# Six layer-1 steps of the fifth and sixth group as 128-token products, and one pair of weight sums placed later

## The chip, the cores and the metric

The kernel runs on one core of a Trainium2 chip. Its metric is the device time of one execution, in microseconds (us), here as a median over several executions. A core has five engines that work side by side, each through its own list of instructions in order: TensorE (PE in the profile, its weight loads PEld), VectorE (DVE), ScalarE (ACT), GpSimd (POOL) and SyncE (SP, which here only starts DMAs). They wait for one another on semaphores.

## The reference

Two layers, one behind the other, over 4 sequences of 768 tokens with 8 heads of 64 features.

```python
# linear attention with decay, in blocks of 64 tokens
intra = einsum('bhic,bhjc->bhij', qb, kb) * Dmask     # lower triangle of lam**(i-j)
intra = einsum('bhij,bhjd->bhid', intra, vb)
inter = einsum('bhid,bhde->bhie', qb * lam_pow, kv_state)
out   = intra + inter
kv_state = lam_block * kv_state + einsum('bhsd,bhse->bhde', kb_dec, vb)
# then, with the heads side by side as x of 512 features
xn = (x - mean) / sqrt(var + 1e-6) * g_ln
y  = x + maximum(xn @ w_ch1, 0) @ w_ch2               # 512 -> 2048 -> 512
```

Inputs and output are float32; the kernel multiplies in bfloat16 and float16 and adds in float32.

## The kernel before

The 3072 tokens are cut into 12 units of 256 tokens, numbered u = 0 to 11. A unit passes through the attention, gives normalised and transposed activations `xT`, and is then a group g = u of the two-layer network (`mlp(g)`, L524). The fifth group is g = 4, the sixth g = 5.

Nothing is ordered by a scheduler. The lower part of the kernel (from L961) is one long list, written by hand, of loads, attention stages and "units": `units(n)` (L1044) takes the next n steps of the list `plan` (L1028 to L1040) and emits them. Each engine executes its share of the list in the order of the text.

*Layer 1.* Group g has eight layer-1 steps. In the usual form, `m1` (L531), a step fills one PSUM bank with two blocks of 128 hidden features for all 256 tokens: 2 blocks times 4 slices of the 512 inputs, 8 products of 128x128 weights with 256 columns (L539), and one ACT instruction that applies the maximum and writes `hT` (L542). In the other form, `m1_tile(c, i)` (L643), a step takes four feature blocks for the 128 tokens of half i: 16 products with 128 columns (L650) and an ACT instruction of the same size (L653). Four tile steps for c in (2, 3) and i in (0, 1) do the work of the last four usual ones. Every product is a weight load and a matmul, two PE instructions.

*Layer 2.* Groups 0 to 3 multiply `hT` by `w2` directly (`m2`, L659: four steps per 128 tokens, four products of 512 columns each at L676), and DVE adds the scaled result to x (`finish`, L700). Groups 4 to 11 replace eight block products by seven (`m2w`, L636, products P1 to P7 into the banks pwa to pwd at L574). These need sums of blocks of W2, which `w_sums(c, n)` (L792) puts into `wt[c]` once for each of the four pieces c of W2: n = 0 gives two of the four sums of a piece (L798, L799), n = 1 the other two (L801, L802), all on DVE. They also need sums of the hidden activations, `h_sums` (L549), again on DVE.

*Attention.* For units 6 to 11 the stage `X(u)` (L943; `X1` and `X2` for u = 6) puts four runs of small 64x64 products one behind the other on PE: `av64` and `inter` of unit u-1, `kv64` and `scores64` of unit u. Unit u's transposed `kqT` and most `xT` come through DMA transposes started by SP.

All PSUM results of the network and of `kv64` share one tag, "mm", with four banks that go round: a product into a bank waits until the instruction that read its last content is done.

Of the kernel before, what the change touches and what calls it, by code (L numbers as in the profile page):

```python
# [17 lines left out]
def kernel(  # L18
# [773 lines left out]
    def w_sums(c, n):  # L792
        v = w2[c].rearrange("p (k e) d -> p k e d", e=2)
        w = DM // 2
        b11, b12, b21, b22 = v[:, :, 0, 0:w], v[:, :, 0, w:], v[:, :, 1, 0:w], v[:, :, 1, w:]
        t1, t2, t3, t4 = (wt[c][:, :, i] for i in range(4))
        if n == 0:
            nc.vector.tensor_tensor(t1, b12, b11, op=ALU.subtract)  # L798
            nc.vector.tensor_tensor(t3, b12, b22, op=ALU.add)  # L799
        else:  # L800
            nc.vector.tensor_tensor(t2, b11, t3, op=ALU.subtract)  # L801
            nc.vector.tensor_tensor(t4, t2, b21, op=ALU.add)  # L802
# [225 lines left out]
    plan = [(m1b, n) for n in range(m1b.count // 2, m1b.count)]  # L1028
    plan += [(m2, i, part) for part in range(KB // 4) for m2, i in ((m2a, 0), (m2a, 1), (m2b, 0))]
    plan += [(m2b, 1, part) for part in range(KB // 4)]  # L1030
    for g in range(2, len(groups)):
        m1, m2 = mlp(g)
        if g == 3:
            plan += [(m1, n) for n in range(4)] + [(m1.tile, c, i) for c in (2, 3) for i in range(2)]
        else:
            plan += [(m1, n) for n in range(m1.count)]
        if g >= WG:
            plan += [(m2.w, n) for n in range(8)]
        else:
            plan += [(m2, i, part) for i in range(len(groups[g])) for part in range(KB // 4)]  # L1040
# [3 lines left out]
    def units(n):  # L1044
        for _ in range(n):
            f, *a = next(steps)
            f(*a)
# [55 lines left out]
    in_v(4, nc.gpsimd)  # L1103
    units(3)
    w_sums(0, 0)
    w_sums(0, 1)
    units(2)
    w_sums(1, 0)
    units(3)
    s12(3)  # L1110
# [265 lines left out]
```

## Time and profile before

| | |
|---|---|
| time before, median of 3 runs | 211.05 us (209.8, 211.05, 211.47) |
| the profiled execution's own time | 209.97 us |
| its span in the profile | 208.3 us |
| PE busy | 197.5 us (95%), 3179 products and as many weight loads |
| DVE, ACT, POOL busy | 136.2 us, 120.8 us, 85.7 us |
| PE clock granted | full in all 40 slices |
| layer-1 products, usual form (L539) | 688 |
| layer-1 products, tile form (L650) | 160 |
| DMA queue q8, instructions | 25 packets, 0.41 MB |

The span is the stretch from the first to the last recorded instruction; the execution takes 1.7 us more. Times within the profile are counted from the start of the span. A busy PE is not a PE at its peak, since the ends of matmuls are modelled: where the text gives a rate of products, it is taken from the starts of two neighbouring runs.

### The profile page before, as it was taken

Reading aid. Unit: us, or ns where it says so; the run is one execution under the profiler, and the core shown is the slowest. Engines: PE = TensorE matmul, PEld = TensorE weight load, DVE = VectorE, ACT = ScalarE, POOL = GpSimd, SP = SyncE. Lnnn points to the kernel's source line nnn. Section 1 sums busy time; section 2 is a strip of 40 time slices with the busy share of each in tenths; the row PEclk is TensorE's granted clock in tenths of the full one; section 3 lists DMA queues with packets and bytes.
Section 4 is the critical chain, followed back from the end, with each engine's and each line's share of the span. In section 5 each row is a group of like instructions: output and inputs, shape, how many; then the busy total and the mean of one; then the engine's idle time right before and its main releaser. Section 6 shows DMA issues by size and latency. Waiting matters only on the chain.

```text
span 208.3 us, 7396 instructions
## 1 busy us (share of the span) xinstructions
PE 197.5 (95%) x3179; PEld 157.9 (76%) x3179; DVE 136.2 (65%) x277; ACT 120.8 (58%) x278; POOL 85.7 (41%) x118
## 2 busy tenths in 40 slices
PE   4989999999999999999999999999799999999991
PEld 2468798454775686588888888888588888888880
DVE  3588543437865659786887874848947947855262
ACT  3776577444466378085665866575486665752620
POOL 5658059118663531663275424753552202011020
PEclk9999999999999999999999999999999999999999
DMA  4999999999899999999899999798995020168303
GB/s 109 301 250 222 177 273 161 206 295 266 206 208 284 219 164 170 185 214 216 179 198 184 191 191 182 198 184 172 195 139 130 6 50 0 30 164 241 127 18 88
DMA packets 91011, 36.41 MB, mean 175 GB/s; under 512 B 65121, under 2 KB 88161, under 8 KB 90978
## 3 DMA queue, kind: packets, MB, share of 16 engines
q1 hardware_dynamic: 86368, 31.53, 75.0%
q0 software_dynamic: 4224, 4.19, 12.9%
q8 instruction: 25, 0.41, 0.8%
q10 hardware_dynamic: 386, 0.20, 0.4%
q14 instruction: 8, 0.07, 0.1%
HBM read 27.27 MB, written 6.29 MB: 161 GB/s over the span
## 4 chain that ended last, share of the span: by engine, by line
PE 81%; DMA 6%; DVE 5%; ACT 2%; POOL 1%; issue 1%; SPq 0%; POOLq 0%; DVEq 0%
PE pm L539 35%; PE pm L676 11%; PE pwd L574 6%; PE pwc L574 6%; PE pwa L574 6%; PE pm1t L650 5%; DMA w<-in_moe_w_ch_dram 4%; PE pwb L574 3%; DMA kin<-in_k_dram 3%; PE po L441 2%; PE po L428 2%; DVE x L587 1%; PE po L415 1%; DVE x L700 1%; PE sc L362 1%; PE xt L502 1%
## 5 line engine op out<-in xcount | busy, mean ns | idle before, releaser
L539 PE MATMUL pm<-xT,w 128*128 128x256 bf16 x688 | 79.4, 273 | 1.8 <-DVE xc L469 1.5
L539 PEld LDWEIGHTS <-w 128*128 128x128 bf16 x688 | 65.9, 98 | 11.1 <-issue 2.2
L542 ACT ACTIVATE hT<-pm 128x512 f16<-128x512 f32 x86 | 50.9, 597 | 31.4 <-PE pm L539 31.3
L676 PE MATMUL pm<-w,hT 128*128 128x512 f16 x128 | 29.8, 380 | 0.0
L574 PEld LDWEIGHTS <-hs 128*128 128x128 f16 x256 | 24.8, 98 | 3.3 <-DVE hs L557 0.3
L599 POOL TENSOR_TENSOR x<-ev_u,x 128x256 f32<-128x256 f32 x8 | 6.0, 749 | 48.0 <-ACT ev_u L598 36.6
L557 DVE TENSOR_TENSOR hs<-hT 128x1024 f16<-128x1024 f16 x16 | 11.0, 690 | 16.8 <-ACT hT L542 16.8
L676 PEld LDWEIGHTS <-hT 128*128 128x128 f16 x128 | 11.7, 98 | 12.5
L574 PEld LDWEIGHTS <-hT 128*128 128x128 f16 x192 | 18.8, 98 | 2.2
L322 POOL TENSOR_TENSOR Sn<-Stmp,lam_s 128x256 bf16<-128x256 f32 x16 | 9.8, 616 | 25.0 <-DVE Stmp L400 14.7
L469 DVE SCALAR_TENSOR_TENSOR xc<-po,nmean,g_row 128x512 bf16<-128x512 f32 x18 | 13.0, 746 | 5.3 <-ACT nmean L468 5.2
L467 ACT ACTIVATE x<-po 128x512 f32<-128x512 f32 x18 | 10.6, 590 | 8.1 <-PE po L441 4.9
L245 POOL TENSOR_TENSOR vb<-vin,lam_p 128x1024 bf16<-128x1024 f32 x6 | 12.0, 1995 | 6.2 <-ACT x L467 3.2
L245 POOL TENSOR_TENSOR vb<-vin,lam_v 128x1024 bf16<-128x1024 f32 (+1 forms) x7 | 11.6, 1660 | 6.0 <-DMA vin<-in_v_dram 6.0
L512 ACT ACTIVATE sq<-x,nmean 128x512 bf16<-128x512 f32 x18 | 12.9, 719 | 0.3
L292 DVE TENSOR_TENSOR mA<-sc,keep 128x512 bf16<-128x512 f32 x14 | 9.0, 684 | 4.6 <-PE sc L282 4.6
L239 POOL TENSOR_TENSOR kq<-qin,lam_p 128x512 bf16<-128x512 f32 x9 | 9.3, 1043 | 4.0 <-PE sc L362 2.5
L650 PE MATMUL pm1t<-xT,w 128*128 128x128 bf16 x160 | 10.5, 228 | 0.2 <-DMA w<-in_moe_w_ch_dram 0.2
L650 PEld LDWEIGHTS <-w 128*128 128x128 bf16 x160 | 9.9, 103 | 0.7 <-DMA w<-in_moe_w_ch_dram 0.5
L587 DVE SCALAR_TENSOR_TENSOR x<-pwd,rstd,x 128x256 f32<-128x256 f32 x16 | 7.7, 482 | 3.4 <-POOL x L607 3.4
L587 DVE SCALAR_TENSOR_TENSOR x<-pwa,rstd,x 128x512 f32<-128x512 f32 (+1 forms) x16 | 9.1, 613 | 0.8
L574 PE MATMUL pwa<-w,hT 128*128 128x256 f16 x64 | 9.6, 273 | 0.0
(134 smaller groups left out, 317.6 us busy)
## 6 DMA issues: line engine op xcount, KB each, us to landing
out_dram<-x SPq DMA_DIRECT2D x22, 256.0 KB, 4.2
w<-in_moe_w_ch_dram POOLq DMA_DIRECT2D x8, 512.0 KB, 8.3
kin<-in_k_dram SPq DMA_DIRECT2D x14, 256.0 KB, 4.9
qin<-in_q_dram SPq DMA_DIRECT2D x14, 256.0 KB, 4.6
vin<-in_v_dram SPq DMA_DIRECT2D x14, 256.0 KB, 5.1
kin<-in_k_dram SPq DMA_DIRECT2D x5, 512.0 KB, 6.2
qin<-in_q_dram SPq DMA_DIRECT2D x5, 512.0 KB, 7.7
vin<-in_v_dram SPq DMA_DIRECT2D x5, 512.0 KB, 7.2
```

The lines of the kernel that those rows point to most:

```text
L245: eng.tensor_tensor(st[u]["vb"][:, hs], qkv_in[u]["v"][:, hs], lv.to_broadcast([128, n, 2, D]), op=ALU.mult)
L322: eng.tensor_tensor(dst, src, lam_s[:, :, None].to_broadcast([128, NP, D]), op=ALU.mult)
L467: nc.scalar.activation(x, po, ACT.Copy, accum_out=sm)
L469: nc.vector.scalar_tensor_tensor(xc, in0=po, scalar=nm, in1=g_row, op0=ALU.add, op1=ALU.mult)
L512: nc.scalar.activation(sq, s["x"][:, ab], ACT.Square, bias=s["nmean"][:, ab:ab + 1], accum_out=ss[:, ab:ab + 1])
L539: nc.tensor.matmul(pm[:, b, :], lhsT=w1[n // W2K][:, kk, (n % W2K) * 128:(n % W2K + 1) * 128], rhs=xT_of[g][:, kk, 0:N], start=(b == 0 and ...
L542: nc.scalar.activation(hT[:, u * NB:(u + 1) * NB, 0:N], pm, ACT.Relu)
L557: nc.vector.tensor_tensor(s13, b[:, :, 1:2, :].to_broadcast([128, n, 2, 128]), b[:, :, 0:4:3, :], op=ALU.subtract)
L574: nc.tensor.matmul(pr[bank], lhsT=lhs(r), rhs=rhs, start=(first and r == 0), stop=(r == KB // 2 - 1), skip_group_check=True)
L587: nc.vector.scalar_tensor_tensor(out, in0=in0, scalar=r[ab], in1=in1, op0=ALU.mult, op1=ALU.add)
L650: nc.tensor.matmul(pm[:, b, :], lhsT=w1[c][:, kk, b * 128:(b + 1) * 128], rhs=xT_of[g][:, kk, i * 128:(i + 1) * 128], start=(b == 0 and kk ...
L676: nc.tensor.matmul(acc[i], lhsT=hT[:, kk, i * 128:(i + 1) * 128], rhs=w2[kk // W2K][:, kk % W2K, :], start=(kk == 0), stop=(kk == KB - 1))
```

## The change

In `plan`, the group g = 4 gets the form that g = 3 has already: its steps 5 to 8 become four tile steps. The group g = 5 keeps six usual steps, and its last two become two tile steps, c = 3 for both halves. The number of steps per group stays eight, so all that `units(n)` counts stays where it was. PE gets 48 products more, with half the columns each.

In the list, `w_sums(0, 1)` goes behind the next two steps. These two are the last layer-2 step of the group g = 1, which ends in a `finish` (L700, the last output addition of the second group), and the first layer-1 step of g = 2.

```diff
         m1, m2 = mlp(g)
-        if g == 3:
+        if g in (3, 4):
             plan += [(m1, n) for n in range(4)] + [(m1.tile, c, i) for c in (2, 3) for i in range(2)]
+        elif g == 5:
+            plan += [(m1, n) for n in range(6)] + [(m1.tile, 3, i) for i in range(2)]
         else:
             plan += [(m1, n) for n in range(m1.count)]
...
     units(3)
     w_sums(0, 0)
+    units(2)
     w_sums(0, 1)
-    units(2)
     w_sums(1, 0)
     units(3)
     s12(3)
```

## The prediction

> **What bounds the kernel.** I read the page's first part and the chain of waits, then the waits of PE, then the timeline at each place where PE stood still.
>
> ```profile
> PE 197.5 (95%) x3179; PEld 157.9 (76%) x3179; DVE 136.2 (65%) x277; ACT 120.8 (58%) x278; POOL 85.7 (41%) x118
> q8 instruction: 25, 0.41, 0.8%
> PE 81%; DMA 6%; DVE 5%; ACT 2%; POOL 1%; issue 1%; SPq 0%; POOLq 0%; DVEq 0%
> ```
>
> PE sets the time, and from 57 us on the chain is nearly all PE. So a change counts by what it adds to PE's work or takes from PE's gaps. There are two gaps worth the name after the start-up, and the change touches both, one of them by accident.
>
> **First gap: 55.06 to 55.44 us.** Timeline of DVE, then of PE (start, duration, instruction, count, idle time before it):
>
> ```profile
> 50.25 1.79 DVE L798 TENSOR_TENSOR wt<-w 128x512 f16<-128x512 f16 x1
> 51.96 0.82 DVE L799 TENSOR_TENSOR wt<-w 128x512 f16<-128x512 f16 x1
> 52.82 0.72 DVE L801 TENSOR_TENSOR wt<-w,wt 128x512 f16<-128x512 f16 x1
> 53.57 1.15 DVE L802 TENSOR_TENSOR wt<-wt,w 128x512 f16<-128x512 f16 x1
> 54.65 0.74 DVE L700 SCALAR_TENSOR_TENSOR x<-pm,rstd,x 128x512 f32<-128x512 f32 x1
> ...
> 52.43 2.78 PE L539 MATMUL pm<-xT,w 128*128 128x256 bf16 x24
> 55.44 1.03 PE L539 MATMUL pm<-xT,w 128*128 128x256 bf16 x8 [0.23 <-DVE x L700]
> ```
>
> The second group's last addition (L700) stands on DVE behind four W2 sums, though its product has been ready since 52.6. It frees the bank that the fourth layer-1 step of g = 2 needs. PE's slot for that step was 52.43 + 24 x 0.1094 = 55.06, so 0.38 us are lost (the 0.23 is counted from a modelled end).
>
> **Second gap: 148.20 to 149.95 us.** Timeline of PE's weight loads, then the busy time of PE, PEld, DVE, ACT, POOL with counts, in two stretches:
>
> ```profile
> 62.56 0.20 PEld L441 LDWEIGHTS <-kqT 64*64 64x64 bf16 x7 [0.42 <-issue]
> 62.97 0.10 PEld L441 LDWEIGHTS <-kqT 64*64 64x64 bf16 x1 [0.21 <-issue]
> 147.41 0.77 PEld L539 LDWEIGHTS <-w 128*128 128x128 bf16 x8
> 149.95 1.64 PEld L539 LDWEIGHTS <-w 128*128 128x128 bf16 x16 [1.76 <-issue]
> 62.97:149.00 86.03, 85.40 (x1533) 69.07 (x1533) 63.71 (x125) 53.19 (x134) 38.89 (x47) 1.00 1.07 196
> 149.00:149.90 0.90, 0.00 (x0) 0.00 (x0) 0.90 (x3) 0.75 (x3) 0.65 (x3) 1.00 0.57 97
> ```
>
> PE's waits put this gap down to DVE's xc (L469), which ends at 149.83. I don't believe it: no layer-1 product reads that xc or its bank, and the same step after the X stages at 117, 132 and 163 us does not wait. It is the weight load, with nothing to wait for ("issue"), that stands still. And the count fits something else. A small halt of 0.2 us lies at 62.97, in the middle of a run of equal products. From there to the gap PE executes 1533 products, 1533 loads and 6 semaphore instructions: 3072 = 12 x 256. The Trainium skill, "Runtime: NRT & Kernel Launch", section "Instruction fetch mechanics", says that each engine's instructions are refilled in 16 KiB blocks of 256 by a DMA queue of its own while the block before is executed. The trace agrees: q8 moved 25 packets of 16 KB, for some 6,370 PE instructions. In the DMA view by narrow windows one packet starts at 147.36, and one at 60.51. So both halts are PE waiting for its next page, 2.6 and 2.5 us after its packet began to move.
>
> That makes the place of the page boundaries in the work decisive. One X stage is 240 to 256 instructions, which PE runs in 1.2 to 1.5 us (from 146.20 to 147.41, 121 products and 120 loads); the same number in layers 1 and 2 takes 13 us. Pages that hold an X stage, by the stretches:
>
> ```profile
> 97.80:102.39 4.59, 4.55 (x129) 3.88 (x130) 3.74 (x9) 2.97 (x9) 1.45 (x2) 1.00 0.92 145
> 113.52:117.28 3.76, 3.76 (x131) 3.24 (x129) 2.67 (x7) 3.44 (x10) 1.16 (x2) 1.00 1.28 142
> 129.68:132.61 2.93, 2.93 (x130) 2.56 (x129) 2.42 (x7) 1.06 (x5) 2.74 (x3) 1.00 0.53 103
> 146.21:149.94 3.73, 2.25 (x129) 1.86 (x128) 3.24 (x9) 2.39 (x9) 1.60 (x4) 1.00 1.10 192
> 162.41:166.02 3.61, 3.61 (x144) 3.31 (x141) 3.12 (x8) 2.55 (x10) 1.35 (x3) 1.00 0.02 5
> ```
>
> A group is 481 to 497 instructions, two pages are 512, so each group's X stage slides back in its page: 4.59, 3.76, 2.93, then 3.73 - 1.75 = 1.98 us to fetch the next page in. With packets at 97.52, 113.61 and 128.92 and 2.5 us to use, the first three were in time by 2.4, 1.2 and 1.2 us; the fourth was 1.75 late. The fifth had idle DMA queues (share 0.02). The Trainium skill, "DMA: Bandwidth & Descriptors", section "Queues, rings and completion order", says an engine serves its queues in turn, packet by packet; that DMA was busy (1.10) is what the trace shows of it.
>
> **The change part by part.**
>
> *The tile steps.* Timeline of PE:
>
> ```profile
> 75.30 3.75 PE L650 MATMUL pm1t<-xT,w 128*128 128x128 bf16 x64
> 78.88 1.03 PE L676 MATMUL pm<-w,hT 128*128 128x512 f16 x4
> 90.69 5.41 PE L539 MATMUL pm<-xT,w 128*128 128x256 bf16 x48
> 95.94 0.93 PE L574 MATMUL pwa<-w,hT 128*128 128x256 f16 x7
> ```
>
> A narrow product takes 3.58/64 = 55.9 ns, a wide one 5.25/48 = 109.4 ns. A step goes from 8 x 109.4 = 875 to 16 x 55.9 = 895 ns; six steps cost +0.12 us, all on PE's path. The skill's "TensorE: Matmul & The Clock Gate", section "Back-to-back issue gap", gives some 81 ns for 128 columns when loads count, and 56 without; this trace shows the 56. ACT's evictions stay (597 ns of either form, inside a step). DVE's activation sums wait for the same last eviction; P1 and P2 need only half 0, so nothing is later there. No DMA is moved.
>
> *The added instructions.* 48 products are 96 instructions, 64 from g = 4, 96 from the end of g = 5. Every boundary then lies so many instructions earlier in the work. X(10) begins at the boundary of 146.21 (page and stage coincide). Afterwards a boundary lies 95 before it, that is 95 x 54.7 ns = 5.2 us of dense products, and the page ends 161 into it: 5.2 + 0.8 = 6.0 us to fetch in, against 3.74 that the late page took from its boundary to use. By the same count the pages up to X(7), X(8), X(9) last 7.5, 8.3 and 7.5 us, and those behind them over 7. X(11)'s is 3.5 + 1.0 = 4.5, with idle queues. The slowest fetch of the trace took 6.1 us (56.91 to 62.97, the small halt); it would fit in each of them but X(10)'s, which it would miss by 0.1 (X(11) apart). So the gap closes: 1.75 less the usual step of 0.05 is -1.70 us. Behind it nothing waits: xT for the next group lands at 154.2 against a use at 163.6, kqT of unit 11 at 157.5 against 162.9, and the DMA share falls to 0.1.
>
> *The moved sums.* L700 starts at 52.78, ends at 53.52, and PE's wait of 0.38 goes. L801 and L802 follow (1.87 at their old pace, to 55.4), then the next pair (1.01, to 56.4); the masks need DVE at 56.74. If that pair ran at the pace of 50.25 (2.61) the masks would slip 1.3 us and the 64x64 products behind them at most 0.5. Nobody reads wt before 96 us. No queue of SP or POOL is passed. But the page halt of 62.97 comes next: if its packet starts when the queues let it and not when PE asks, that halt grows by what PE gained. Ends: 0 and -0.38; I take -0.25. kqT of unit 3 lands at 54.84 against 56.3, that of unit 7 at 101.64 against 102.0, so both still hold.
>
> Sum against the profiled execution: 209.97 + 0.12 - 1.70 - 0.25 = 208.14. Its own time lies 1.08 under the median. If that spread is the halt's (a race of one DMA), the new median is 208.1; if it is unrelated, 211.05 - 1.83 = 209.2. I take 208.6, nearer the first.
>
> **Rivals.**
>
> *The halt stays or moves (0.25).* Xc really was the releaser, or another boundary gets a slow packet. For: the page names DVE, to 0.12 us; X(10)'s margin is 0.1. Against: the count of 12 x 256. Then 211.05 + 0.12 - 0.25 = 210.9, within 1%.
>
> *Loads set the pace of the narrow products (0.05).* At g = 4 and 5 each of the 96 is held to the 98 ns of its load (PEld's own duration) or the skill's 81 ns: 96 x 81 - 48 x 109.4 = +2.5, at 98 ns +4.2 us. From 75 ns on it eats the gain. 211.05 - 1.95 + 4.2 = 213.3, slower. Against: 55.9 ns in 64 such products with loads from the same w1.
>
> *PE earlier than kqT of unit 7 (0.05).* SP sets its landing at 101.64; a slip of 1 us costs 0.6, to 209.2, and more is not in sight.
>
> **How the numbers follow.** The forecast has 0.65. About 1% is what a measurement of this kernel can tell from no change: under 208.9 is faster. Of the forecast's chance some 0.5 lies there, the rest and the first rival are the same, and slower holds the load rival and what I don't see. The range goes from 207.4 (no spread, and both small halts gone) to 210.8, nearly the halting case.
>
> **What would show it.** After: no "issue" gap of a microsecond at PEld near 147 to 150; q8 with 25 or 26 packets; L650 x256 and L539 x640; tile runs at 56 ns; L700 directly behind L799 at 52.8 and no PE wait for it; a halt at 62.6 to 63.0 of 0.2 to 0.6. Wrong would be a gap elsewhere at a multiple of 256 instructions from 62.97, or one at the same place of the work.

## The result and the profile after

| | before | after |
|---|---|---|
| median | 209.93 us (208.37 to 212.61, 22 runs) | 208.92 us (207.85 to 210.3, 22 runs) |
| ratio to before | | 0.9948, 95% interval 0.9926 to 0.997 |
| profiled execution, its span | 209.97, 208.3 us | 208.6, 206.9 us |

The change makes the kernel 0.5% faster, clear of noise and inside the 1% that was to count as no change. Ratios, here and below, leave out executions that took over 1.5% more than the fastest of their kernel. With 22 runs the kernel before stands at 209.93, not at the 211.05 of the first three.

The page after (busy time by engine, the instruction queue, the chain by engine):

```profile
PE 197.6 (96%) x3227; PEld 159.3 (77%) x3227; DVE 133.6 (65%) x277; ACT 120.7 (58%) x278; POOL 84.7 (41%) x118
q8 instruction: 25, 0.41, 0.9%
PE 86%; DMA 6%; DVE 2%; ACT 1%; POOL 1%; issue 1%; SPq 0%; POOLq 0%; DVEq 0%
```

48 more products and the same busy time of PE. DVE's share of the chain has fallen from 5% to 2% and ACT's from 2% to 1%: the chain no longer passes through them at the two gaps, which are gone. Timeline after, of DVE and PE at the first gap, then of PE's weight loads at the two page halts (start, duration, instruction, count, idle time before it):

```profile
50.80 0.73 DVE L798 TENSOR_TENSOR wt<-w 128x512 f16<-128x512 f16 x1
51.46 0.83 DVE L799 TENSOR_TENSOR wt<-w 128x512 f16<-128x512 f16 x1
53.18 0.75 DVE L700 SCALAR_TENSOR_TENSOR x<-pm,rstd,x 128x512 f32<-128x512 f32 x1 [0.89 <-PE pm L676]
53.84 1.21 DVE L801 TENSOR_TENSOR wt<-w,wt 128x512 f16<-128x512 f16 x1
55.09 0.42 DVE L802 TENSOR_TENSOR wt<-wt,w 128x512 f16<-128x512 f16 x1
...
52.98 3.66 PE L539 MATMUL pm<-xT,w 128*128 128x256 bf16 x32
...
62.72 0.20 PEld L441 LDWEIGHTS <-kqT 64*64 64x64 bf16 x7 [0.42 <-issue]
63.36 0.10 PEld L441 LDWEIGHTS <-kqT 64*64 64x64 bf16 x1 [0.44 <-issue]
147.74 3.28 PEld L539 LDWEIGHTS <-w 128*128 128x128 bf16 x31
```

The last addition (L700) now waits only for its own product, and four layer-1 steps run as one piece of 32 products where 24 and 8 stood. The halt at 63 us has grown. And behind X(10), from 147.74 on, the loads run through without a gap.

Where the profiled time went, by the start of the same work in the two timelines:

| work | before | after | lead gained since the row above |
|---|---|---|---|
| first layer-1 step, g = 2 | 52.43 | 52.98 | -0.55 (start-up, no edit) |
| fifth layer-1 step, g = 2 | 57.23 | 57.39 | +0.39 (moved sums) |
| layer-2 step behind the halt | 63.12 | 63.51 | -0.23 (longer halt) |
| P1, g = 4 | 95.94 | 96.38 | -0.05 (four tile steps, and 0.03 regained) |
| P1, g = 5 | 110.79 | 111.27 | -0.04 (two tile steps) |
| layer 1 behind X(10) | 147.42 | 147.74 | +0.16 (not traced) |
| P1, g = 8, the next after it | 156.07 | 154.74 | +1.65 (page gap) |

Start-up apart this is a gain of 1.88 us in one pair of profiles. Over all executions the gain is smaller: by the ratio 0.52% or 1.1 us (interval 0.6 to 1.6).

### The profile page after: what moved, and what is told of

It reads as the page before. It is cut to its first block, busy times and chain, and to the rows that moved or that the text cites. A ratio compares the mean times of both kernels' runs of the same rounds, so it can differ in the third digit from the quotient of the medians.

```text
span 206.9 us, 7492 instructions
## 1 busy us (share of the span) xinstructions
PE 197.6 (96%) x3227; PEld 159.3 (77%) x3227; DVE 133.6 (65%) x277; ACT 120.7 (58%) x278; POOL 84.7 (41%) x118
## 4 chain that ended last, share of the span: by engine, by line
PE 86%; DMA 6%; DVE 2%; ACT 1%; POOL 1%; issue 1%; SPq 0%; POOLq 0%; DVEq 0%
PE pm L539 34%; PE pm L676 14%; PE pm1t L650 8%; PE pwd L574 6%; PE pwa L574 6%; PE pwc L574 6%; DMA w<-in_moe_w_ch_dram 4%; PE pwb L574 3%; DMA kin<-in_k_dram 3%; PE po L441 2%; PE po L428 2%; DVE x L587 1%; PE po L415 1%; PE sc L362 1%; PE xt L502 1%; PE sc L282 1%
## 5 line engine op out<-in xcount | busy, mean ns | idle before, releaser
L539 PE MATMUL pm<-xT,w 128*128 128x256 bf16 x640 | 73.7, 273 | 0.0
L539 PEld LDWEIGHTS <-w 128*128 128x128 bf16 x640 | 61.4, 98 | 8.2 <-DVE Smid L397 0.3
L542 ACT ACTIVATE hT<-pm 128x512 f16<-128x512 f32 x80 | 47.2, 597 | 29.0 <-PE pm L539 28.8
L557 DVE TENSOR_TENSOR hs<-hT 128x1024 f16<-128x1024 f16 x16 | 12.7, 795 | 15.8 <-ACT hT L542 14.5
L574 PEld LDWEIGHTS <-hT 128*128 128x128 f16 x192 | 18.7, 98 | 2.1
L650 PE MATMUL pm1t<-xT,w 128*128 128x128 bf16 x256 | 16.3, 225 | 0.2 <-DMA w<-in_moe_w_ch_dram 0.2
L650 PEld LDWEIGHTS <-w 128*128 128x128 bf16 x256 | 15.4, 101 | 0.9 <-DMA w<-in_moe_w_ch_dram 0.4
L653 ACT ACTIVATE hT<-pm1t 128x512 f16<-128x512 f32 x16 | 9.3, 595 | 4.9 <-PE pm1t L650 4.9
```

The source lines that it names most:

```text
L539: nc.tensor.matmul(pm[:, b, :], lhsT=w1[n // W2K][:, kk, (n % W2K) * 128:(n % W2K + 1) * 128], rhs=xT_of[g][:, kk, 0:N], start=(b == 0 and ...
L542: nc.scalar.activation(hT[:, u * NB:(u + 1) * NB, 0:N], pm, ACT.Relu)
L557: nc.vector.tensor_tensor(s13, b[:, :, 1:2, :].to_broadcast([128, n, 2, 128]), b[:, :, 0:4:3, :], op=ALU.subtract)
L574: nc.tensor.matmul(pr[bank], lhsT=lhs(r), rhs=rhs, start=(first and r == 0), stop=(r == KB // 2 - 1), skip_group_check=True)
L650: nc.tensor.matmul(pm[:, b, :], lhsT=w1[c][:, kk, b * 128:(b + 1) * 128], rhs=xT_of[g][:, kk, i * 128:(i + 1) * 128], start=(b == 0 and kk ...
```

## The experiments

The edits are against the kernel before unless they say otherwise, and the ratios are to it. A "page" is a block of 256 of PE's instructions, as the prediction has it. "Edge" is the boundary of two pages, a place 193 + 256k in PE's list of products, loads and semaphore instructions, counted in each trace; "gap" is the distance between the starts of the two instructions around it; packets are those of q8, each with the instructions of one page.

**Two halves of the change.** The moved sums alone are the second part of the diff above; the tile steps alone are the first.

> The kernel before with the moved pair of W2 sums alone; PE's list is the same, so its page boundaries too. Page theory: the halt in the middle of the 64x64 products at 63 us grows by what PE gained (to about 0.5), the gap of about 1.7 us inside the first layer-1 steps after X(10) is there as in the kernel before, 3072 instructions behind the small halt; time within 0.3 us of before. Rival (the gap of 148 us waits for DVE's xc): the same here. Rival (the sums give the whole gain of the change): 0.5% faster.

> The kernel before with the six tile steps alone. Page theory: no gap at PE's weight loads after X(10), although nothing of that stage, its waits or DVE's order is changed; six steps cost 0.12 us together; the time is that of the changed kernel within 0.3 us, about 0.5% under before. The wait of 0.4 us on the second group's last addition stays. Rival (xc is the releaser): the gap of 1.7 us is still there and the time is 0.1 us over before.

The sums alone: 1.0007 (0.9982 to 1.0032). The tile steps alone: 0.9962 (0.9937 to 0.9986). Timeline of PE's loads, of the sums alone at both edges, then of PE's loads, of DVE and of PE with the tile steps alone, the first two behind X(10), the last at the first layer-1 steps of g = 2:

```profile
63.45 0.10 PEld L441 LDWEIGHTS <-kqT 64*64 64x64 bf16 x1 [0.39 <-issue]
147.88 0.77 PEld L539 LDWEIGHTS <-w 128*128 128x128 bf16 x8
150.14 0.88 PEld L539 LDWEIGHTS <-w 128*128 128x128 bf16 x9 [1.49 <-issue]
...
149.11 1.97 PEld L539 LDWEIGHTS <-w 128*128 128x128 bf16 x19
150.77 1.40 DVE L469 SCALAR_TENSOR_TENSOR xc<-po,nmean,g_row 128x512 bf16<-128x512 f32 x2
53.83 3.66 PE L539 MATMUL pm<-xT,w 128*128 128x256 bf16 x32
```

With the sums alone both halts stand at the old instructions, and the one at 63 us is 0.47 where it was 0.29. With the tile steps alone the gap behind X(10) is gone, though nothing that X(10) reads, writes or waits for was touched, and PE is past its eighth layer-1 product long before xc begins at 150.77. This rules out xc as the releaser.

The last line contradicts what I expected of the tile steps alone: the wait for L700 was to stay, as its cause is still in the list, but the four layer-1 steps run as one piece. The same holds for every other profile of a kernel with the sums in the old place: 80, 208 and 256 start-up instructions, the later v, the later q of unit 9 and the kernel before once more, all below. One profile of eight has the wait, the first one. So in most executions seen the moved sums had nothing to gain, which fits the ratio of 1.0007.

The profile of the tile steps alone has a wait of another kind. Timeline of PE, POOL and DVE behind X(8):

```profile
121.50 5.41 PE L539 MATMUL pm<-xT,w 128*128 128x256 bf16 x48 [0.49 <-DVE Smid L397]
119.37 1.04 POOL L239 TENSOR_TENSOR kq<-qin,lam_p 128x512 bf16<-128x512 f32 x1 [3.63 <-PE pwd L574]
120.37 0.61 POOL L322 TENSOR_TENSOR Sn<-Stmp,lam_s 128x256 bf16<-128x256 f32 x1
121.02 0.42 DVE L397 TENSOR_TENSOR Smid<-pk,Sn 128x256 f32<-128x256 f32 x1 [1.50 <-POOL Sn L322]
```

No edge lies there. The third layer-1 step needs a bank that Smid frees, Smid needs Sn, and Sn stands on POOL behind the scaling of unit 9's q. A later test takes this up.

**Forty start-up products, no part of the change.** Then the same with the moved sums.

```diff
-    for _ in range(16):
+    for _ in range(36):
         for b in range(2):
             nc.tensor.matmul(unread[half[b]], ...)
```

> The kernel before with 40 more of the small start-up products that nobody reads (80 PE instructions, beside waits of PE on the first loads). No tile step, no moved sum. Page theory: all boundaries lie 80 instructions earlier in the work, the gap after X(10) is gone and the halt at 63 us too; 0.5% to 0.9% faster than before. Rival (xc, or something in the tile steps themselves): the gap stays, the time is that of before.

> The moved pair of sums and the 40 start-up products, no tile step. Page theory: both page halts are gone, so that the gain of the moved sums (0.38 us) is no longer taken back at 63 us, and the 0.12 us of the tile steps are saved: 0.3 to 0.6 us faster than the changed kernel, some 0.7% to 1% under before. Rival (tile steps matter by themselves): not faster than before by more than 0.2%.

The products alone: 0.9955 (0.9934 to 0.9977), a little less than expected. With the sums: 0.9938 (0.9922 to 0.9955), less than expected too. Timeline of PE's loads behind X(10) with the products alone, then of PE and its loads with the sums as well:

```profile
148.12 2.95 PEld L539 LDWEIGHTS <-w 128*128 128x128 bf16 x28
...
53.61 3.66 PE L539 MATMUL pm<-xT,w 128*128 128x256 bf16 x32
62.13 0.22 PEld L441 LDWEIGHTS <-kqT 64*64 64x64 bf16 x8
```

Eighty instructions that compute nothing give as much as the tile steps. This is the main proof: what matters of the 48 products more is that they are 96 instructions. In both kernels the eight loads at the old halt run as one, and so do the four layer-1 steps, with the sums moved or not. The difference of 0.17% between the two, and that of 0.1% to the changed kernel, lie inside the intervals. The 40 products are not free at the start: a gap of 1.7 to 2.0 us opens at an edge at 15 us, mostly beside the wait for W1 that ends at 16.3 us in the kernel before. The first layer-1 product comes at 17.3 and 17.1 us, against 16.3 to 17.1 in the profiles without these products.

**Other numbers of start-up products.** The same edit with range(68), 208 instructions, and range(80), 256, exactly a page.

> The kernel before with 104 more of the small start-up products that nobody reads: 208 PE instructions, nothing else. All page boundaries lie 208 instructions earlier in the work. Page theory: the gap after X(10) is gone, and by the same count the short pages are now those that hold X(7) and X(8) (2.2 and 2.1 us from boundary to boundary without a gap), so that gaps of 0.3 to 1.7 us appear there, near 102 and 118 us, at instructions 193 + 256k of PE's list; the time is near that of before, within 0.5%. Rival (any more start-up products help by themselves, or xc is the releaser): as fast as with 80 instructions, or a gap at the old place.

> The kernel before with 128 more small start-up products: 256 PE instructions, one page exactly, so that every boundary of the later work lies where it lay before. Page theory: the halt at 63 us and the gap of 1 to 1.8 us in the first layer-1 steps after X(10) are both back at the same work; the time is that of before within 0.4%, not the 0.45% less that 80 instructions gave. Rival (the start-up products themselves are what helps): as fast as with 80, or faster.

208: 1.0073 (1.0046 to 1.0099). 256: 1.0111 (1.0016 to 1.0206). Timeline of 208, PE and its loads, then of 256, loads:

```profile
93.10 0.38 PE L362 MATMUL sc<-kqT 64*64 64x64 bf16 x22 [0.51 <-issue]
138.28 0.75 PEld L539 LDWEIGHTS <-w 128*128 128x128 bf16 x7 [0.91 <-issue]
...
149.50 0.77 PEld L539 LDWEIGHTS <-w 128*128 128x128 bf16 x8
151.75 0.77 PEld L539 LDWEIGHTS <-w 128*128 128x128 bf16 x8 [1.49 <-issue]
```

With a whole page the gap is back, eight products into the layer-1 steps behind X(10), 1.48 us long. With 208 it has left X(10); two others, 0.70 and 1.01 us, are at edges, one in the middle of X(6)'s scores and one behind X(9). I had named X(7) and X(8), the two shortest pages. So the count says where a halt can be, but which page is late depends on its packet. Both expectations on the time missed. The many products themselves delay the start, the first layer-1 product comes at 18.7 and 18.4 us instead of 16.3; that this is all of the missing time is not shown. The 256 were executed only four times.

**Less DMA traffic ahead of the late page.** `load_in(11, "v")` moves behind the two `to_xT(9, ...)`.

> The kernel before, PE's list untouched; only the load of unit 11's v is issued on SP behind the transposes of unit 9's xT, some 6 us later, so that less DMA traffic lies before the page of X(10). Page theory: the boundary stays where it is, but the page's packet starts sooner than 147.36 and the gap shrinks by as much, to between 0 and 1.2 us. Rival (xc is the releaser): the gap is 1.7 us as before, since DVE's order and PE's are the same. If the packet does not start sooner, the gap stays under the page theory too, and this run tells nothing apart.

1.0023 (0.9998 to 1.0048). Timeline of PE's loads behind X(10), then of DVE behind X(8):

```profile
151.77 1.32 PEld L539 LDWEIGHTS <-w 128*128 128x128 bf16 x13 [1.12 <-issue]
122.22 0.42 DVE L397 TENSOR_TENSOR Smid<-pk,Sn 128x256 f32<-128x256 f32 x1 [3.05 <-POOL Sn L322]
```

The packet starts 0.57 us after PE crosses the edge instead of 1.15, and the gap is 1.11 us instead of 1.75. That fits, but it is not clean. In the four other profiles that keep this page and the old order of loads, the packet starts 0.74 to 1.38 us after the edge, so 0.57 is only just outside. And in this execution PE came to X(10) 2.5 us later, held at X(8) by unit 9's q.

**Unit 9's q behind X(8) on POOL.** In three kernels, `in_q_one(9, nc.gpsimd, 0)` goes behind `X(8)` and the unit after it: with the sums and 40 products, with the changed kernel, with the kernel before.

> The moved sums and the 40 start-up products, and on POOL the first half of unit 9's q is scaled behind X(8) instead of ahead of it. Theory of a second wait: after X(8) the third layer-1 step needs a bank that DVE's Smid frees, DVE waits for POOL's Sn, and Sn stands behind that q, whose load lands late in some executions; with the q behind, DVE's Smid never waits for Sn there and the slow tail of the times goes: 0.1 to 0.4 us faster than without the swap, some 0.8% to 1% under before. Rival (page halts are all there is): equal to the 0.62% without the swap within 0.15%.

> The changed kernel with the same swap on POOL. Theory of a second wait: 0.1 to 0.4 us faster than the changed kernel (ratio 0.993 to 0.994 against before instead of 0.9948), no wait of Smid on Sn near 119 us. Rival (page halts are all there is): ratio 0.995.

> The kernel before with the swap alone; PE's list and its pages stay. Theory of a second wait: 0.1 to 0.5 us faster than before, the gap of 1.1 to 1.8 us after X(10) stays. If the median gains 0.3 us or more, that wait held a good part of what the medians of before lose. Rival (page halts are all there is): as before within 0.2%.

0.9942 (0.9919 to 0.9965), 0.9932 (0.9905 to 0.9959) and 0.9998 (0.9977 to 1.0018), against 0.9938, 0.9948 and 1 without it. Timeline of DVE, changed kernel with the swap; then, for the kernel before with the swap, PE's loads behind X(10) and the busy time of PE, PEld, DVE, ACT and POOL behind that gap, with the granted clock:

```profile
118.39 0.42 DVE L397 TENSOR_TENSOR Smid<-pk,Sn 128x256 f32<-128x256 f32 x1
120.00 0.42 DVE L397 TENSOR_TENSOR Smid<-pk,Sn 128x256 f32<-128x256 f32 x1
...
151.36 5.71 PEld L539 LDWEIGHTS <-w 128*128 128x128 bf16 x38 [2.14 <-issue]
151.36:155.16 3.80, 3.80 (x20) 2.78 (x21) 0.75 (x2) 1.60 (x3) 3.23 (x3) 0.55 0.42 77
```

Smid does not wait for Sn in the three profiles with the swap, but neither did it in the changed kernel's own, and the times don't move beyond their intervals. The wait exists in single executions (0.5 and 2.0 us of PE); as a part of the medians it is not shown, and that theory falls.

The kernel before with the swap shows something else. Its gap behind X(10) is 2.13 us, more than the 1.1 to 1.8 expected. Behind it the granted clock is 0.55 for 3.8 us, in which 20 products run where 35 would fit at 109.4 ns. That execution took 212.95 us. So a late page can be followed by a second loss as large as the gap; that the halt itself brings the clock down is likely, but not shown.

**The page of the kernel before restored inside the changed kernel.** Against the changed kernel:

```diff
             pm = mm_tile([128, NB, N], F32, "pm1")
+            if g == 6 and u == 0:
+                for i in range(80):
+                    r, b = half[0], half[i % 2]
+                    nc.tensor.matmul(pm[b, 0, 0:32], lhsT=ident[r, b], rhs=ident[r, 0:32], ...)
```

> The changed kernel, tile steps and moved sums included, with 80 small products that nobody reads at the start of the first layer-1 step of the seventh group (near 118 us): 160 PE instructions, which with the 96 of the tile steps make one page, so that from there on every boundary lies at the work where it lay in the kernel before. Page theory: a gap of 1.1 to 2.1 us at PE's weight loads is back 16 instructions into the layer-1 steps after X(10), its packet 2.5 us ahead of its end; the products themselves cost 1 to 2 us of PE; the time is 1% to 2% over that of the changed kernel. Rival (the tile steps or the sums removed what xc was waited for): no gap there, 0.5% to 1% over the changed kernel.

1.0258 (1.0196 to 1.0319). Timeline of PE's loads at the added products and behind X(10), then the busy time of PE, PEld, DVE, ACT and POOL with the granted clock behind it (lines are 4 further down in this kernel: L539 is the added product, L543 the layer-1 product):

```profile
118.40 0.99 PEld L539 LDWEIGHTS <-ident 64*64 64x64 bf16 x58 [0.21 <-issue]
121.21 0.60 PEld L539 LDWEIGHTS <-ident 64*64 64x64 bf16 x22 [1.81 <-issue]
152.69 0.88 PEld L543 LDWEIGHTS <-w 128*128 128x128 bf16 x9
154.60 3.48 PEld L543 LDWEIGHTS <-w 128*128 128x128 bf16 x32 [1.03 <-issue]
...
121.84:126.00 4.16, 4.16 (x30) 3.20 (x27) 0.00 (x0) 1.19 (x2) 0.00 (x0) 0.65 1.23 162
```

With tile steps and moved sums in place, the gap behind X(10) is back (1.13 us), because the page is. The added products make a short page of their own, and PE stops among them for 1.89 us: 57 of 80 equal products, then nothing, with no semaphore in sight. A third halt of 0.62 us lies at the end of X(9). The time, of four executions, is worse than I expected. In the profile the granted clock fell to 0.65 in the 4.16 us behind the long halt; by estimate 4.16 x 0.35 = 1.5 us went there.

**The kernel before once more,** one execution of 210.52 us.

> The kernel before once more, for a second look at the sizes. Page theory: halt at 63 us of 0.1 to 0.6, gap after X(10) of 1.1 to 2.1 us, each at the same instructions of PE's list; the sizes follow the packets and need not be those of the first profile.

```profile
150.59 1.43 PEld L539 LDWEIGHTS <-w 128*128 128x128 bf16 x14 [1.44 <-issue]
```

The gap is 1.43 us and the halt at 64 us 0.09, at the same instructions. Gaps of the profiles taken together:

| kernel | gaps at edges behind the start-up | packet to PE's next instruction |
|---|---|---|
| before | 0.29, 1.75 | 2.46, 2.59 |
| before again | 0.09, 1.43 | 2.41, 2.66 |
| sums alone | 0.47, 1.48 | 2.68, 2.72 |
| v later | 0.41, 1.11 | 2.53, 2.53 |
| before, unit 9's q later | 2.13 | 2.74 |
| 256 start-up instructions | 0.15, 1.48 | 2.69, 2.47 |
| 208 start-up instructions | 0.70, 1.01 | 2.56, 2.43 |
| after, page restored | 1.89, 0.62, 1.13 | 2.80, 2.46, 2.70 |
| after | 0.52 | 2.52 |
| after, unit 9's q later | 0.10 | 2.47 |

The tile steps alone and the three kernels with 40 start-up products have none. The last column is the signature: whatever the gap, PE goes on 2.4 to 2.8 us after the packet begins. And what the profile names is not stable. In the kernel before it was xc, in the sums alone, with 256 instructions and in the kernel before once more Smid, among the added products "issue". In the kernel before it is the instruction that happened to end 0.12 us before PE went on.

## Why the prediction was right, and where its sizes were off

*The boundaries.* Right, by four runs that change nothing but PE's count (80, 208 and 256 start-up instructions, and the restored page). X(10)'s page lasts 6.03 us after the change, from 141.21 to 147.24, as the 6.0 that was worked out, and its packet came in time: it starts at 140.01.

*The size of that term.* 1.70 us was one sample. In the six profiles that keep the page of the kernel before, the gap is 1.75, 1.43, 1.48, 1.11, 1.48 and 2.13, on average 1.56; less the 0.05 between two products anyway, 1.51 are lost. The prediction took the gap of one profile for the typical one, and it came out somewhat too large.

*The moved sums.* This is the term that was mis-sized most. In the pair of profiles it came out: L700 left the path as forecast (0.39 against 0.38), the second pair took 1.21 + 0.42 = 1.63 us against 1.87, and the masks did not slip. But the step "PE's wait of 0.38 goes" took the wait for a fixed part of the kernel before, and seven of eight profiles with the sums in the old place don't have it. "That halt grows by what PE gained" is not shown either. With the sums moved the halt at 63 us is 0.52, 0.47, 0.10 and, with the page restored, none; without, it is 0.29, 0.09, 0.41, with 256 instructions 0.15, and with the tile steps alone or the later q none. So the term is nearer to nothing than to 0.25, and the ratio of the sums alone, 1.0007, cannot tell it from nothing.

*The tile steps.* 3.57/64 and 1.79/32 give 55.8 and 55.9 ns for a product, by the timeline of PE after:

```profile
92.81 3.74 PE L650 MATMUL pm1t<-xT,w 128*128 128x128 bf16 x64
96.38 0.93 PE L574 MATMUL pwa<-w,hT 128*128 128x256 f16 x7
109.48 1.95 PE L650 MATMUL pm1t<-xT,w 128*128 128x128 bf16 x32
111.27 0.93 PE L574 MATMUL pwa<-w,hT 128*128 128x256 f16 x7
```

So +0.12 us stands, and the load rival is out.

*The sum.* With 1.51 for the gap and nothing for the sums it is 0.12 - 1.51 = -1.4 us, inside the measured 0.6 to 1.6 but on its far side. The 208.6 came out close to 208.92 with some luck: it started between two bases, and the base moved down by 1.1. Faster by over 1%, which had a chance of about 0.5, did not come true; it leaned on the high median of three runs.

*What stays open.* Tile steps alone and start-up products alone gained 0.4% and 0.45%, 0.8 and 0.9 us, less than the 1.4 that the gaps of the profiles would give. Their intervals just reach to 1.3 and 1.4. Whether the gap is shorter in the other executions is not known, since no trace of them is kept.

## What to carry to other kernels

When PE stands still at an instruction that waits for nothing, in the middle of equal ones, count its instructions from one such place to the next. Here a multiple of 256 pointed to instruction fetch, and the releaser that the profile named was a coincidence. A dense run of small products can use up a page faster than the next one comes: X(10)'s page takes 1.98 us without its gap, and the packet alone needs 2.4 to 2.8. So where the page boundaries lie against such a run was worth about a microsecond here, and any edit upstream that changes the count moves them. Test a supposed gain of such an edit against a few instructions that do nothing, before the edit itself is given the credit. And look at more than one profile before a wait is priced: of the two gaps of the first profile, one stood in every profile with that page, the other in one of eight.

## What was not expected of the hardware

Where PE halted at an edge, it went on 2.4 to 2.8 us after the packet had begun, though behind X(10) the packet itself took 0.9 to 1.3 us. In the profiles with the gap there, it began 0.4 to 1.4 us after PE had crossed X(10)'s edge, with the DMA share at 1.10 in the kernel before. In two profiles the granted clock fell right behind a halt: to 0.55 over 3.8 us after 2.13 us behind X(10), and to 0.65 over 4.2 us after 1.89 us among the added small products. Behind the other gaps of the table, up to 1.75 us, it stayed at 1.00.
